# A fill of spare scratch rows moved to the end of attention, another order of that end, and twenty products of ones ahead of the first expert

## The chip, the core and the metric

The kernel runs on one core of one Trainium2 chip. The metric is the time of one execution on the device in microseconds (us), lower being better; it is given as the median of several executions. Inside the core, TensorE (PE in the views, with PEld for its weight loads), VectorE (DVE), ScalarE (ACT) and GpSimd (POOL) compute, each from an instruction queue of its own; SyncE (SP) only issues transfers here. Sixteen DMA engines carry the transfers.

## The reference

Three stages, each fed by the one before. Cut to what matters:

```python
# 1. attention as a chunked scan: batch 4, heads 8, length 768, head size 32, state 16, chunk 32
for c in range(24):
    L = np.exp(cum[..., :, None] - cum[..., None, :]) * causal
    M = np.einsum('bhin,bhjn->bhij', Cc, Bc) * L
    y[:, :, sl] = einsum(M, xc) + einsum(Cc, state) * exp(cum)
    state = decay_full * state + sum_j(Bx)
x = y.transpose(0, 2, 1, 3).reshape(3072, 256)          # 3072 tokens of 256 values
# 2. and 3. two layers of 8 experts; each token goes to the one expert of its largest logit
for e in range(8):
    h = np.maximum(x[mask_e] @ w1[e], 0.0)               # 256 -> 1024
    out[mask_e] = gate_w[mask_e, None] * (h @ w2[e])     # 1024 -> 256
```

The first layer takes its logits from normalised tokens and expert embeddings, the second from `x @ w_gate`.

## The kernel before

**Attention.** The work is cut into eight "quads" q = 0..7 (two for each batch, four heads each). A quad has an `intra` part (products within a chunk, three groups of them), a state part, and an `inter` part (what the states add, again three groups, the last step of each being the copy of `y` from PSUM to `yT`). One Python program writes all instructions in an order made by hand: quad q's `intra` is interleaved with quad q-1's `inter`, and generators (`run(gen, n)` advances one by n steps) put other work between. An engine runs its own instructions in the order in which they were written; semaphores order the engines against each other.

**Routing.** `batch_route` computes the gate of one batch, or of half a batch, and calls `route`: on PE the rank of each token in its expert ("rk" tiles, a sum over `cum`, the running count by expert), on DVE the slot number `idx` and the new `cum`, and on POOL one indirect DMA for each 128 tokens (L218), which scatters 266-word rows to the slots of the expert in DRAM scratch: `scr1` for the first layer, `scr2` for the second. The `idx` tiles have two buffers. At the end of attention there are four such halves: `p0` and `p1` of batch 2, `parts[0]` and `parts[1]` of batch 3.

**Fills.** Slots that no token reaches must hold an id out of range. `prefill` (L259) writes the tile `zrow` over them by DMAs on SP: `scr1` in the quad q = 1, `scr2` in q = 2 to 5. For each expert of `scr2` there are two blocks: 384 rows (399 KB) and behind them 256 overflow rows (266 KB). `scr2` gets its first scatter in the first layer.

**End of attention and early block.** The first 162 rows of expert 0 (`early1`, tiles ending in m0a) go through the first layer in plain f32 while attention ends: transposes, eight products h0 to h7, then y0 and y1, its gate and its rank `rkm0a`. `counts` (L239) sums `cum` by a PE product `cntm`; its program position is behind the last rank of batch 3.

**First layer.** `xrm` is the load of expert 0's other 270 rows from `scr1` (L279); it waits for all scatters to `scr1`. Then PE transposes these rows (`xT0m`, `xT1m`, L289), ACT and DVE split them into a high and a low part (`xhm`, `xlm`), and each weight product is made of three (L308 for h, L330 for y). The experts follow one after another, then the second layer in the same way. `wsplit` (L120 on ACT, L121 on DVE) splits a weight tile; `wload` issues weight loads on SP.

Of the kernel before, what the change touches and what calls it, by code (L numbers as in the profile page):

```python
# [9 lines left out]
F32 = mybir.dt.float32  # L10
# [10 lines left out]
NTOK, D, E, F = NB * S, 256, 8, 1024  # L21
# [7 lines left out]
C2P, C2T, X2T = 128, 3, 2  # L29
R1 = NTOK + 384  # L30
R2 = NTOK + 512
# [5 lines left out]
def ssm_moe_moe_kernel(  # L37
# [20 lines left out]
    pe, dve, act, pool, sp = nc.tensor, nc.vector, nc.scalar, nc.gpsimd, nc.sync  # L58
# [8 lines left out]
    scr2 = dram.tile([E * R2, W], F32, name="scr2")  # L67
# [22 lines left out]
    def wload(upto):  # L90
        while wpos["load"] < min(upto, len(pieces)):
            i = wpos["load"]
            m, e, which, k = pieces[i]
            if m == 1 and e < NEE and which == 0:
                raw = fpool[0].tile([128, WP], F32, name=f"raw{i}")
            else:
                raw = wpool0.tile([128, WP], F32, tag="raw", name=f"raw{i}", bufs=3)
            sp.dma_start(raw, wsrc[m][which][e, :, k * WP:(k + 1) * WP])
            wraw[i] = raw
            if m == 1 and e < NEE and which == 0:  # L100
                eraw[e].append(raw)
            wpos["load"] += 1
# [26 lines left out]
    ones = const.tile([128, 128], BF16, name="ones")  # L129
# [126 lines left out]
                reason="rows come from all scatters",  # L256
            )

    def prefill(scr, r, blocks, es):  # L259
        for e in es:  # L260
            o = e * r
            for pn, n in blocks:
                sp.dma_start(
                    scr[o:o + pn * n, :].rearrange("(p t) w -> p t w", t=n),
                    zrow[:pn].to_broadcast([pn, n, W]),
                )
                o += pn * n
# [253 lines left out]
    with ExitStack() as actx:  # L521
# [30 lines left out]
        def load_br(b):  # L552
            t = fil_p.tile([128, 4, NCH, NS], F32, tag="brt", name=f"brt{b}")
            sp.dma_start(t, br[b])
            return t
# [83 lines left out]
        def fil(n):  # L639
            for _ in range(n * rate):  # L640
                next(fil_gen, None)
                run(side, 1)
                run(router, steps)
# [3 lines left out]
        def warm(n):  # L647

            nwarm[0] += 1
            p = psC.tile([128, 512], F32, tag="c", name=f"pw{nwarm[0]}")  # L650
            for _ in range(n):
                pe.matmul(p, lhsT=wz[:, :128], rhs=wz, start=True, stop=True)
# [33 lines left out]
        def quad_p(q):  # L686

            b, hq = divmod(q, 2)
            p = psC.tile([128, 512], F32, tag="c", name=f"pp{q}")
            pe.matmul(p[:, :384], lhsT=selA[64:128, 128 * b:128 * b + 128],  # L690
                      rhs=asp[64:128, 384 * hq:384 * hq + 384], start=True, stop=True,
                      tile_position=(64, 0))
            pv = p[:, :384].rearrange("p (v i) -> p v i", i=CH)
            if q == NQ - 2:
                return pv
            t = au.tile([128, 6, CH], F32, tag="pt", name=f"pt{q}")
            act.copy(t, pv)
            return t

        def quad_c(q, r):  # L700

            pr = slice(32 * r, 32 * r + 32)
            eng = pool if q in (1, 2, 3) else dve
            eng.tensor_tensor(cxb[q % 2][pr, :, r, :], cxs[q][pr], pts[q][pr], ALU.mult)

        def quad_f(q):
            fb = au.tile([128, NS, NCH], F32, tag="fb", name=f"fb{q}")
            act.copy(fb, ft[:, q:q + 1, :].to_broadcast([128, NS, NCH]))
            return fb
# [20 lines left out]
        def quad_state(q, us, fb):  # L730
            st = au.tile([128, NS, NCH], F32, tag="st", name=f"st{q}", bufs=1)
            dve.tensor_tensor_scan(
                st[:].rearrange("p n c -> p (n c)"), fb[:].rearrange("p n c -> p (n c)"),
                us[:].rearrange("p n c -> p (n c)"), 0.0, op0=ALU.mult, op1=ALU.add,
            )
            sx = au.tile([128, NCH, 2, NS], F32, tag="sx", name=f"sx{q}")
            sv = st[:].rearrange("p n c -> p c n")
            act.activation(sx[:, :, 0, :], sv, AF.Copy, scale=hmask[:, 0:1])
            dve.tensor_scalar(sx[:, :, 1, :], sv, hmask[:, 1:2], None, op0=ALU.mult)
            return sx  # L740

        def quad_transpose(q, sx):
            ss = au.tile([128, 3, 128], F32, tag="ss", name=f"ss{q}")
            p = psC.tile([128, 512], F32, tag="c", name=f"sT{q}")
            for g in range(3):
                pe.transpose(
                    p[:, 128 * g:128 * g + 128],
                    sx[:, 4 * g:4 * g + 4].rearrange("p c h n -> p (c h n)"), ident[:]
                )
            pv = p[:, :384].rearrange("p (g m) -> p g m", m=128)  # L750
            act.copy(ss[:, 0:1], pv[:, 0:1])
            act.copy(ss[:, 1:], pv[:, 1:])
            return ss
# [58 lines left out]
        def run(gen, n=None):  # L812

            while gen is not None and (n is None or n > 0):
                if next(gen, "end") == "end":
                    return
                n = None if n is None else n - 1
# [210 lines left out]
        for q in range(1, NQ - 2):  # L1028
            b, hq = divmod(q, 2)
            rate = 2 if q == 1 else 1  # L1030
            steps = 2
            cur = Quad(q)
            if q == 1:
                prefill(scr1, R1, [(C1P, C1T)], range(4))
                pts[0] = quad_p(0)
                for r in range(4):
                    quad_c(0, r)
                warm(2)
                fil(1)
                run(cs)  # L1040
                warm(2)
                pend.fb = quad_f(0)
            sx = quad_state(q - 1, pend.us, pend.fb)
            cur.intra(0)
            fil(1)
            pts[q] = quad_p(q)
            pend.ss = quad_transpose(q - 1, sx)
            fil(1)
            if q + 3 < NQ and q > 1:
                halves[q + 3] = expand_half(q + 3, raws[q + 3])  # L1050
            quad_c(q, 3)
            if q + 4 < NQ and q > 1:
                raws[q + 4] = load_half(q + 4)
            fil(1)
            if q == 1:
                halves[4] = expand_half(4, raws[4])
                raws[5] = load_half(5)
            quad_c(q, 1)
            cxs[q + 1] = cxs.get(q + 1) or load_cx(q + 1)
            pend.inter(0)  # L1060
            quad_c(q, 2)
            cur.fb = quad_f(q)
            pend.inter(1)
            fil(1)
            quad_c(q, 0)
            xts[q + 1] = dma_x(q + 1)
            if q < NQ - 3:
                fil(2)
            cur.intra(2)
            pend.inter(2)  # L1070
            if hq == 0:
                run(router)
                rows = new_rows(b - 1)
                router = batch_route(b - 1, (yTs[q - 2], yTs[q - 1]), rows, 0, NT, 5)
            fil(3 if q < NQ - 3 else 0)
            if hq == 0 and b + 2 < NB:
                brs[b + 2] = load_br(b + 2)
            cur.intra(1)
            if q == 1:
                prefill(scr1, R1, [(C1P, C1T)], range(4, 8))  # L1080
            else:
                prefill(scr2, R2, [(C2P, C2T), (C2P, X2T)], ((0, 1), (2, 3, 4), (5, 6), (7,))[q - 2])
            pend = cur

        q = NQ - 2
# [21 lines left out]
        early = early1()  # L1107
# [15 lines left out]
        run(p0, 1)  # L1123
        quad_c(q + 1, 3)
        wload(7)
        run(p0, 1)
        c6.inter(1)
        c7 = Quad(q + 1)
# [20 lines left out]
        run(p0)  # L1149
        c7.inter(1)  # L1150
        run(p1, 1)
        run(early, 1)
        run(p1, 2)
        c7.inter(2)
        rows = new_rows(NB - 1, act.copy)
        parts = [
            batch_route(NB - 1, (yTs[NQ - 2], yTs[NQ - 1]), rows, t0, t0 + 3) for t0 in (0, 3)
        ]
# [3 lines left out]
        run(p1, 1)  # L1162
        run(parts[0], 3)
        run(p1)
        run(early, 1)
        run(parts[1], 2)
        run(parts[0], 1)
        run(early, 1)
        run(parts[1], 1)
        run(early, 1)  # L1170
        run(parts[0], 1)
        run(parts[1], 1)
        run(parts[0])
        run(early, 2)
# [16 lines left out]
    with ExitStack() as c1:  # L1191
        psM = c1.enter_context(tc.tile_pool(name="psM", bufs=2, space=PSUM))
# [46 lines left out]
        prev = route(C0P, C0T, None, va0[:C0P], 1, rows0[:C0P], scr2, E * R2, scats2, psM, "m0a")  # L1239
        for _ in prev:  # L1240
            pass
        for k in range(KD):
            x_split_k(xr, pn, nt, xs, k, psM, "c", "m0")

# [4 lines left out]
        for e in range(E):  # L1249
            tag = f"m{e}"  # L1250
# [64 lines left out]
    psM = ctx.enter_context(tc.tile_pool(name="psM2", bufs=2, space=PSUM))  # L1315
# [5 lines left out]
    for e in range(E):  # L1321
        tag = f"n{e}"
# [95 lines left out]
```

## Time and profile before

| what | value |
|---|---|
| median of 3 executions | 503.15 us (501.55, 503.15, 503.8) |
| the profiled execution | 503.57 us, its span 501.9 us |
| granted TensorE clock, mean | 0.968 |
| PE busy | 460.2 us (92%) in 3207 instructions |
| PE weight loads | 410.9 us (82%) |
| DVE busy | 287.1 us (57%) |
| ACT busy | 239.7 us (48%) |
| POOL busy | 138.5 us (28%) |
| fill DMAs `scr<-zrow` | 8 of 448.9 KB, 8 of 399.0 KB, 8 of 266.0 KB |

The span runs from the first to the last instruction of the profiled execution; the 1.67 us between it and that execution's time lie around it. Busy shares are means over stages that differ. The granted clock is PE's share of full speed: 1.00 is 2.4 GHz, 0.5 is 1.2 GHz.

### The profile page before, as it was taken

To read this page: it belongs to the slowest core of one execution; us is meant where nothing else is said; L and a number is where in the kernel's file an instruction comes from. 1 tells how busy PE (TensorE), PEld (TensorE's weight loads), DVE (VectorE), ACT (ScalarE), POOL (GpSimd) and SP (SyncE) were. 2 spreads that over 40 slices of the span, in tenths; PEclk is the share of its full clock that TensorE was granted. 3 is DMA by queue.
4 is the path that set the end of the run, shared out by engine and by line. 5 is a ranking of instruction groups with operands and counts; after the bars stand their busy time and mean duration, and the time that the engine had idled before them with its cause. 6 is when DMAs were issued, how large, how long until landed. Compare 5 with 4: busy or idle time off the path is not lost.

```text
span 501.9 us, 8953 instructions
## 1 busy us (share of the span) xinstructions
PE 460.2 (92%) x3207; PEld 410.9 (82%) x3209; DVE 287.1 (57%) x682; ACT 239.7 (48%) x558; POOL 138.5 (28%) x211
## 2 busy tenths in 40 slices
PE   8889987989759999999999999899999999999992
PEld 3555754767659999999999999789999999999991
DVE  6977775787736837456383746543666357244330
ACT  5542533556625644547364545344556346344330
POOL 6334465155830030321303030511101210212011
PEclk9997978989979999999999999999999999999997
DMA  7267899586224535252433535252754564411000
GB/s 247 84 189 195 219 214 260 131 259 208 77 87 138 194 100 194 84 178 101 154 128 111 168 110 194 71 153 92 236 183 153 170 229 145 131 39 60 22 22 16
DMA packets 50212, 72.09 MB, mean 144 GB/s; under 512 B 23870, under 2 KB 36093, under 8 KB 49899
## 3 DMA queue, kind: packets, MB, share of 16 engines
q1 hardware_dynamic: 45595, 61.66, 41.2%
q0 software_dynamic: 4560, 9.70, 5.8%
q8 instruction: 32, 0.52, 0.4%
q14 instruction: 25, 0.20, 0.1%
HBM read 52.53 MB, written 19.74 MB: 144 GB/s over the span
## 4 chain that ended last, share of the span: by engine, by line
PE 47%; DMA 21%; issue 13%; DVE 9%; POOL 3%; ACT 2%; POOLq 1%; SPq 1%; another core or an unknown queue 1%; DVEq 0%; ACTq 0%
DMA out_dram<-os0n,idsn 13%; PE y1m L330 7%; PE y0m L330 7%; DMA out_dram<-os0n1a,idsn1a 6%; PE cb L604 4%; DVE lt L581 2%; PE h0m L308 2%; PE y L759 2%; PE h1m L308 2%; PE h6m L308 2%; PE h2m L308 2%; PE h7m L308 2%; PE h5m L308 2%; PE h3m L308 2%; PE h4m L308 2%
## 5 line engine op out<-in xcount | busy, mean ns | idle before, releaser
L218 POOL DMA_INDIRECT scr<-rows2m,idxm x31 | 31.4, 1014 | 129.8 <-DVE cum L215 106.4
L121 DVE TENSOR_TENSOR w0l<-raw,w0h 128x1024 fp32r<-128x1024 f32 x30 | 36.7, 1224 | 10.2 <-ACT w0h L120 10.2
L121 DVE TENSOR_TENSOR w1l<-raw,w1h 128x1024 fp32r<-128x1024 f32 x30 | 36.4, 1218 | 0.9 <-ACT w1h L120 0.9
L604 PE MATMUL cb<-cw,btt 128*128 128x256 f32 x96 | 32.4, 445 | 1.7 <-ACT btt L549 0.8
L218 POOL DMA_INDIRECT scr<-rows,idxa x24 | 26.4, 1098 | 20.4 <-DVE cum L215 10.3
L120 ACT CAST w1h<-raw 128x1024 fp32r<-128x1024 f32 x30 | 31.5, 1052 | 0.0
L437 POOL DMA_INDIRECT out_dram<-os0n,idsn x8 | 7.8, 969 | 85.6 <-DVE idsn L431 44.6
L120 ACT CAST w0h<-raw 128x1024 fp32r<-128x1024 f32 x30 | 31.2, 1042 | 0.0
L581 DVE TENSOR_TENSOR_SCAN lt<-ab,ipat 128x512 f32<-128x512 f32 x24 | 29.2, 1219 | 1.7 <-PE ab L578 1.5
L312 DVE SCALAR_TENSOR_TENSOR hln<-h0n,hhn 128x384 fp32r<-128x384 f32 (+1 forms) x8 | 4.2, 524 | 43.8 <-ACT hhn L311 39.9
L611 DVE TENSOR_TENSOR mb<-cb,lt 128x256 f32<-128x256 f32 x48 | 18.0, 417 | 14.4 <-PE cb L604 8.5
L604 PEld LDWEIGHTS cb<-cw,btt 128*128 128x128 f32 x96 | 18.0, 212 | 10.0 <-PE y L759 2.3
L330 PE MATMUL y1m<-hhm,w1h 128*128 128x432 f32 (+1 forms) x64 | 23.0, 360 | 0.0
L330 PE MATMUL y0m<-hhm,w1h 128*128 128x432 f32 (+1 forms) x64 | 22.9, 358 | 0.0
L312 DVE SCALAR_TENSOR_TENSOR hlm<-h0m,hhm 128x432 fp32r<-128x432 f32 (+1 forms) x8 | 4.7, 587 | 31.6 <-issue 23.4
L330 PE MATMUL y0m<-hhm,w1l 128*128 128x432 f32 (+1 forms) x64 | 22.4, 349 | 0.0
L330 PE MATMUL y1m<-hhm,w1l 128*128 128x432 f32 (+1 forms) x64 | 22.3, 349 | 0.0
L330 PE MATMUL y0m<-hlm,w1h 128*128 128x432 f32 (+1 forms) x64 | 22.3, 348 | 0.0
L330 PE MATMUL y1m<-hlm,w1h 128*128 128x432 f32 (+1 forms) x64 | 22.3, 348 | 0.0
L592 POOL TENSOR_TENSOR mb<-brt,lt 128x128 f32<-128x128 f32 x24 | 10.6, 440 | 40.3 <-DVE lt L581 35.7
L335 ACT COPY ytm<-y1m 128x432 f32<-128x432 f32 (+1 forms) x8 | 4.0, 502 | 31.8 <-PE y1m L330 31.8
L716 PEld LDWEIGHTS y<-mb,xbd 128*64 128x64 f32 x384 | 15.8, 145 | 4.0 <-issue 2.1
(607 smaller groups left out, 1568.6 us busy)
## 6 DMA issues: line engine op xcount, KB each, us to landing
raw<-in_m2w_dram SPq DMA_DIRECT2D x32, 512.0 KB
raw<-in_m1w_dram SPq DMA_DIRECT2D x28, 512.0 KB
scr<-zrow SPq DMA_DIRECT2D x8, 448.9 KB
scr<-zrow SPq DMA_DIRECT2D x8, 399.0 KB
xrm<-scr SPq DMA_DIRECT2D x7, 448.9 KB
xrn<-scr SPq DMA_DIRECT2D x6, 399.0 KB
xbd<-in_xs__dram SPq DMA_DIRECT2D x24, 96.0 KB
scr<-zrow SPq DMA_DIRECT2D x8, 266.0 KB
```

Of the source, the lines that this page charges most:

```text
L120: act.copy(hi[:, sl], raw)
L121: dve.tensor_tensor(lo[:, sl], raw, hi[:, sl].bitcast(F32), ALU.subtract)
L218: i = pool.indirect_dma_start(out=scr[:], out_offset=bass.IndirectOffsetOnAxis(ap=idx[:pn, t, :], axis=0), in_=rows[:, t, :W], in_offset=None,
L308: pe.matmul(p[:, :n], lhsT=w[:, o:o + 128], rhs=x[:, kd, :n], start=(k == 0), stop=(k == 5))
L312: dve.scalar_tensor_tensor(hl[:, f, :n], p[:, :n], 0.0, hh[:, f, :n].bitcast(F32), op0=ALU.max, op1=ALU.subtract,)
L330: pe.matmul(p[:, :n], lhsT=w[:, o:o + 128], rhs=h[:, f, :n], start=(k == 0), stop=(k == 3 * KF - 1))
L581: dve.tensor_tensor_scan(lts[b, g][:, 2 * v:2 * v + 2].rearrange("p u c i -> p (u c i)"), p, ipat[:].rearrange("p c i -> p (c i)"), 0.0, o ...
L592: pool.tensor_tensor(m[:, :, :, 64:80], brs[b][:, us_, 4 * g:4 * g + 4], lt[:, us_, :, CH - 1:CH].to_broadcast([128, 2, 4, NS]), ALU.mult,)
L604: pe.matmul(p[:, cc], lhsT=btt[:, c].rearrange("p h j -> p (h j)"), rhs=ctt[:, :, c * CH:(c + 1) * CH], start=True, stop=True)
L611: dve.tensor_tensor(mbs[2 * b + hq, g][:, :, o:o + 2, :64].rearrange("p u c i -> p c u i"), p[:, :, us_, :], lts[b, g][:, us_, o:o + 2, :] ...
L716: pe.matmul(yps[g][64 * hs:64 * hs + 64, r * 80:r * 80 + 80], lhsT=xts[hs][:, c, :], rhs=mbs[q, c // 4][:, hs, c % 4, :], start=(r == 0), ...
L759: pe.matmul(yps[g][64 * hs:64 * hs + 64, :320].rearrange("p (c w) -> p c w", w=80)[:, :n, :64], lhsT=ss[:, g, 64 * hs:64 * hs + 64], rhs=c ...
```

## The change

Three edits. The 256-row block of all eight experts of `scr2` is no longer filled in quads 2 to 5, but in one go behind `wload(7)`. At the end of attention `c7.inter(2)` comes before two steps of `p1`, two steps of the early block go, and two steps (of the early block and of `parts[0]`) change places. And twenty products of ones, whose result nothing reads, stand on PE behind `rkm0a` and ahead of the transposes of `xrm`.

```diff
-    def prefill(scr, r, blocks, es):
+    def prefill(scr, r, blocks, es, first=0):
         for e in es:
-            o = e * r
+            o = e * r + first
...
-                prefill(scr2, R2, [(C2P, C2T), (C2P, X2T)], ((0, 1), (2, 3, 4), (5, 6), (7,))[q - 2])
+                prefill(scr2, R2, [(C2P, C2T)], ((0, 1), (2, 3, 4), (5, 6), (7,))[q - 2])
...
         wload(7)
+        prefill(scr2, R2, [(C2P, X2T)], range(E), C2P * C2T)
         run(p0, 1)
...
         run(p1, 1)
-        run(early, 1)
+        c7.inter(2)
         run(p1, 2)
-        c7.inter(2)
         rows = new_rows(NB - 1, act.copy)
...
         run(p1)
-        run(early, 1)
         run(parts[1], 2)
         run(parts[0], 1)
         run(early, 1)
         run(parts[1], 1)
+        run(parts[0], 1)
         run(early, 1)
-        run(parts[0], 1)
         run(parts[1], 1)
...
+        p = psM.tile([128, 4, 128], F32, tag="a", name="pw")
+        for _ in range(20):
+            pe.matmul(p, lhsT=ones, rhs=ones[:].unsqueeze(1).to_broadcast([128, 4, 128]),
+                      start=True, stop=True)
         for k in range(KD):
             x_split_k(xr, pn, nt, xs, k, psM, "c", "m0")
```

On SP, in quad 3 (the names: `xbd` is x of a quad, `cxt` its C, `scr_69` the second layer's scratch), before the change:

```order
L680 DMA xbd_121<-in_xs__dram 64x12x32 x2
L263 DMA scr_69<-zrow 384x1x266
L263 DMA scr_69<-zrow 256x1x266
L263 DMA scr_69<-zrow 384x1x266
L263 DMA scr_69<-zrow 256x1x266
L263 DMA scr_69<-zrow 384x1x266
L263 DMA scr_69<-zrow 256x1x266
L564 DMA cxt_1032<-in_cx_dram 128x384
L680 DMA xbd_122<-in_xs__dram 64x12x32 x2
```

With the change only the three blocks of 384 rows stay between the loads of x and of C. The others stand on SP behind the weight loads of the end of attention (`raw` is a weight tile; `xrm0a` is the load of the early block, `xrm` that of expert 0's other rows):

```order
L279 DMA xrm0a<-scr_68 81x532
L98 DMA raw_1382<-in_m1w_dram 128x1024
L98 DMA raw_1384<-in_m1w_dram 128x1024
L98 DMA raw_1386<-in_m1w_dram 128x1024
L263 DMA scr_69<-zrow 256x1x266 x8
L279 DMA xrm_1823<-scr_68 90x798
```

Before the change `xrm` stood directly behind the third weight load.

On PE, where attention ends, the order before (`rka_3` is the rank of `parts[1]`, `cntm` the sum of `cum`, the rest the early block):

```order
L197 MATMUL rka_3_1720<-oha_3_1712,tri 128x24
L378 MATMUL h6m0a<-xm0a,cw 128x162 x2
L378 MATMUL h7m0a<-xm0a,cw 128x162 x2
L242 LDWEIGHTS ones
L242 MATMUL cntm_1753<-cum_79,ones 1x8
L244 LDWEIGHTS ones
L244 MATMUL cntm_1753<-hole_86,ones 1x8
L389 MATMUL y0m0a<-hm0a,cw 128x162 x8
```

And with the change:

```order
L197 MATMUL rka_3_1712<-oha_3_1704,tri 128x24
L378 MATMUL h4m0a<-xm0a,cw 128x162 x2
L378 MATMUL h5m0a<-xm0a,cw 128x162 x2
L242 LDWEIGHTS ones
L242 MATMUL cntm_1745<-cum_79,ones 1x8
L244 LDWEIGHTS ones
L244 MATMUL cntm_1745<-hole_86,ones 1x8
L378 MATMUL h6m0a<-xm0a,cw 128x162 x2
L378 MATMUL h7m0a<-xm0a,cw 128x162 x2
L389 MATMUL y0m0a<-hm0a,cw 128x162 x8
```

The early block has fallen two h products back: h6 and h7, which stood ahead of `cntm`, now stand behind it. The orders of DVE and POOL are the same in both kernels; on ACT the last copies of `y` to `yT` come ahead of the exponentials of `p1`. The twenty products of ones stand on PE between `rkm0a` and the first transpose of `xrm`, each with a weight load of its own.

## Rows read from the trace of the kernel before

**Rows 1.** The page: granted TensorE clock in 40 slices.

```profile
PEclk9997978989979999999999999999999999999997
```

**Rows 2.** Windows: from:to, length, busy by engine (instructions), clock, DMA share, GB/s.

```profile
core 0: us, PE busy (x) PEld busy (x) DVE busy (x) ACT busy (x) POOL busy (x), PEclk, DMA share, GB/s
77.00:83.00 6.00, 2.82 (x22) 1.60 (x18) 1.28 (x3) 1.47 (x5) 3.95 (x5) 1.00 1.14 239
83.00:91.00 8.00, 7.59 (x51) 5.34 (x52) 7.05 (x13) 3.91 (x15) 1.77 (x4) 0.79 1.02 252
124.00:131.00 7.00, 5.63 (x48) 4.91 (x47) 5.41 (x35) 4.47 (x18) 5.95 (x7) 1.00 0.22 82
131.00:139.00 8.00, 6.02 (x43) 5.58 (x44) 5.88 (x13) 4.72 (x9) 6.63 (x8) 1.00 0.24 85
139.00:145.00 6.00, 1.28 (x8) 0.98 (x7) 0.88 (x7) 0.33 (x1) 2.89 (x7) 0.72 0.42 115
145.10:148.50 3.40, 3.40 (x14) 3.21 (x15) 1.27 (x3) 0.80 (x3) 0.89 (x5) 0.50 0.18 68
148.50:152.00 3.50, 3.50 (x31) 3.50 (x31) 2.62 (x5) 3.50 (x8) 0.00 (x0) 1.00 0.02 5
```

**Rows 3.** Timeline of PE, DVE and ACT around 80 us: start, busy, [idle before <-releaser].

```profile
79.18 0.60 PE L604 MATMUL cb<-cw,btt 128*128 128x256 f32 x2
83.41 1.78 PE L759 MATMUL y<-cxb,ss 128*64 128x256 f32 x8 [3.21 <-ACT ss L751]
...
82.66 0.76 DVE L611 TENSOR_TENSOR mb<-cb,lt 128x256 f32<-128x256 f32 x2 [4.16 <-remote]
...
82.62 0.48 ACT L697 COPY pt<-pp 128x384 f32<-128x384 f32 x1 [1.19 <-remote]
```

**Rows 4.** Timeline of SP, the issues of transfers.

```profile
69.96 4.71 SPq L263 DMA_DIRECT2D scr<-zrow  x6
77.21 5.21 SPq L680 DMA_DIRECT2D xbd<-in_xs__dram  x4
...
116.12 1.29 SPq L98 DMA_DIRECT2D raw<-in_m1w_dram  x3
...
140.65 2.38 SPq L279 DMA_DIRECT2D xrm<-scr  x2
```

**Rows 5.** Timeline of POOL: the scatters.

```profile
73.47 1.25 POOL L218 DMA_INDIRECT scr<-rows,idxa  x1 [0.73 <-DMA scr<-zrow]
...
80.44 0.97 POOL L218 DMA_INDIRECT scr<-rows,idxa  x1 [0.30 <-issue]
...
126.84 0.98 POOL L218 DMA_INDIRECT scr<-rows,idxa  x1 [0.30 <-issue]
...
133.66 1.96 POOL L218 DMA_INDIRECT scr<-rows,idxa  x1 [0.30 <-DVE w0l L121]
...
137.20 0.97 POOL L218 DMA_INDIRECT scr<-rows,idxa  x1 [0.30 <-issue]
```

**Rows 6.** The chain that ended last, at 137 us: the last scatter's flight.

```profile
137.20 3.12 DMA scr<-rows,idxa
```

**Rows 7.** Timeline of DVE: the slot numbers of the last half batch.

```profile
130.08 0.18 DVE L206 TENSOR_REDUCE idxa<-psa 128x3 int32<-128x24 f32 x1
```

**Rows 8.** Who waited for scatters of the tile `idxa` from 120 to 140 us (us, times).

```profile
  DVE idxm0a L206: 0.8, 1
```

**Rows 9.** Timeline of PE from 129 to 150 us.

```profile
129.25 0.71 PE L378 MATMUL h7m0a<-xm0a,cw 128*128 128x162 f32 x4
130.68 0.17 PE L242 MATMUL cntm<-cum,ones 128*1 128x8 bf16 x1 [0.71 <-DVE cum L215]
130.87 2.47 PE L389 MATMUL y0m0a<-hm0a,cw 128*128 128x162 f32 x16
139.00 0.18 PE L197 MATMUL rkm0a<-ohm0a,tri 81*81 81x16 bf16 x1
143.90 0.68 PE L289 MATMUL xT0m<-ident,xrm 90*128 90x90 f32 x3 [4.71 <-DMA scr<-rows,idxm0a]
149.11 0.29 PE L308 MATMUL h3m<-xhm,w0h 128*128 128x270 f32 x1
```

**Rows 10.** Timeline of PE at the start: products of 512 columns.

```profile
1.30 4.43 PE L652 MATMUL pw<-wz 128*128 128x512 bf16 x11 [1.30 <-DVE wz L826]
6.33 1.25 PE L652 MATMUL pw<-wz 128*128 128x512 bf16 x5
```

## The prediction

> **What bounds the kernel now.** I began with the page's line of granted clock [rows 1]. PE is the engine with most work, and its clock is near full in all slices but one inside and some in attention, so the time is made of PE's work plus the places where PE stands still. What the change touches ends by about 150 us of the span; behind that PE is busy without a gap until the last expert, so whatever is won or lost up to the start of the first expert's steady products (h3 at 149.11 [rows 9]) is won or lost at the end, one to one.
>
> I then cut the stretches that the change touches into windows [rows 2]. Two are weak. From 77 to 83 us PE is busy 2.82 of 6 us, DVE 1.60, ACT 1.47, while the DMA share is 1.14, which is more than full. From 139 to 145 us PE is busy 1.28 of 6 us: attention has ended and the first expert's rows aren't there yet. The timeline says what each engine waited for. Around 80 us [rows 3] DVE waits 4.16 us and ACT 1.19 us for something that the profile can only call remote, and PE 3.21 us for ACT. At the same time SP needs 5.21 us to issue four small loads, just behind six fills that took 4.71 us to issue [rows 4], and POOL sends six scatters between 73.47 and 81.41 us [rows 5]. So three compute engines, SP and the queues stand together, in the one place where fills and scatters meet. At 140 us the order is simpler: the last scatter is issued at 137.20 and flies 3.12 us [rows 6], to 140.32; `xrm` is loaded from 140.65 [rows 4], and its transposes start at 143.90 after 4.71 us of idle PE [rows 9]. The clock has dropped by then: 0.50 in the window 145.10 to 148.50, 1.00 from 148.50 [rows 2].
>
> **Part 1: the fill moves.** Eight DMAs of 266 KB, 2.13 MB, leave quads 2 to 5; three of quad 3's six go. Its fills come to 3 x 399 = 1.20 MB in place of 1.20 + 0.80 = 2.00 MB. At the 239 GB/s of the window [rows 2] the 0.80 MB are 3.3 us of transfer, and the queue in front of the scatters and loads is that much shorter. What the stall is worth: by PE its 3.21 us of idle [rows 3], and a little more in front of it, since the products at 79.18 end at 79.78 and the next work starts at 83.41, 3.63 us later. By DVE at most 4.16 us, of which it would have waited some anyway, since PE's products that feed L611 end at 79.78 and it restarts at 82.66: 2.88 us. I take 3.3 us, between 2.9 and 3.6; the clock at 0.79 behind the stall [rows 2] speaks for the upper half. Below, this term is nothing, if the stall doesn't come from the amount of fill; the row nearest to it, 3.3 us of transfer gone against 3.3 us of stall, speaks for all of it. **Term: -3.3 us.** The Trainium skill, "SBUF — State Buffer", section "SBUF: two separate sides", speaks against this: the engines' ports and the DMA ports of SBUF can't contend with each other. By it the engines were held by something else than the fill's traffic and this term is 0; the trace, with three engines, SP and the queues standing at once, leaves that open, and it is the first rival.
>
> The fill now stands on SP behind three weight loads that took until 117.41 to issue [rows 4]. Ahead of it nothing is late; behind it on SP stands only `xrm`, which can't go before 140.65 anyhow. Issuing six fills took 4.71 us, so eight take some 6.3 us, and 2.13 MB at 239 GB/s take 8.9 us: until about 132 us if the weights land near 123. That ends 8 us ahead of `xrm`, and the window 124 to 131 has a DMA share of 0.22 [rows 2], so there is room. The first scatter to `scr2` comes behind `rkm0a`, so it doesn't wait.
>
> What is late is the scatters to `scr1` that fly meanwhile. DVE's slot numbers of `parts[1]`, at 130.08 [rows 7], write the tile that `p1`'s scatters read (two buffers); the last of these starts at 126.84 [rows 5] and with a flight of 3.12 us [rows 6] lands at 129.96. So the slack is 0.12 us, and the same wait shows as 0.8 us one route later [rows 8]. A scatter that shares the queues with the fill lands later. Below that is 0; above, the 4.16 us that DVE stood in the crowded window [rows 3]. I take half, **2.1 us**. DVE is then 2.1 us late at L206, and the new `cum` behind it too. The last scatters themselves have 3.6 us in hand: they start at 133.66 at the earliest, behind the others in POOL's queue and behind a weight split of DVE [rows 5].
>
> **Part 2: the order.** Two h tiles, h6 and h7, fall behind `cntm`, which waits for `cum` (0.71 us, at 130.68 [rows 9]). In the kernel before they lay in DVE's shadow. A pair of them costs 0.71 us [rows 9], and pipelined 1.25 us for both by my estimate. So between `cntm` and y0, which start at 130.68 and 130.87, stand 1.25 us more. From there to the end of `rkm0a`, 139.00 + 0.18 = 139.18, the early block's steps follow from each other, with PE 6.02 us busy of 8 from 131 to 139 [rows 2]. `rkm0a` then ends at 139.18 + 1.25 = 140.4, or with the late L206 at 142.5. The other moves change PE alone at places where POOL and DVE set the pace (POOL 5.95, DVE 5.41 of 7 us in 124 to 131): nothing, at most 0.3 us either way.
>
> **Part 3: the ones.** The rows at the start of the kernel have the same shape: five in 1.25 us, 0.25 us each with the last one's way through the array in it, and eleven in 4.43 us, 0.40 us each [rows 10]. 512 columns at 2.4 GHz are 0.213 us; I take 0.217 for a warm PE, **20 x 0.217 = 4.34 us**, and the second row as the bound, 20 x 0.40 = 8.1 us, if PE's clock is low there. Where `rkm0a` ends at 139.18 they would fit into the 4.71 us of idle [rows 9] at no cost. But it ends at 140.4 or 142.5, and they run to 144.7 or 146.85, past 143.90. What they give: the clock doesn't drop. From 143.90 to h3 took 5.21 us (149.11 - 143.90). The 3.40 us in the window at 0.50 would take 1.70 at full clock, so 3.5 us. h3 then starts at 144.7 + 3.5 = 148.2 (0.9 us earlier) without the delay, at 146.85 + 3.5 = 150.35 (1.2 us later) with it. The point where it turns is transposes at 145.6. **Term: +1.2 us.**
>
> **The sum** against the profiled execution, 503.57 us (0.42 above the median of the runs shown): 503.57 - 3.3 + 1.2 = 501.5 us. A run differs from the median by up to 1.6 us, so I call 0.5%, 2.5 us, what can be told from no change.
>
> **The rivals.**
> 1. The stall at 80 us stays, as the SBUF page's rule would have it: the scatters or the loads of x, both still there, hold the engines. For it: only some of the stretches with crowded queues show this wait, and 1.20 MB of fill are still in the queue. Against: it begins as the fills have been issued and ends as the share falls. 503.57 + 1.2 = 504.8 us. Chance 0.20.
> 2. The stall goes, and the scatters land on time, since the share at 124 to 131 is only 0.22 and a scatter is small: 503.57 - 3.3 - 0.9 = 499.4 us. Chance 0.26.
> 3. The stall stays and the scatters land on time: 503.57 - 0.9 = 502.7 us. Chance 0.12.
> 4. Slower: the stall moves with the fill. 2.13 MB now meet the scatters of `p0`, `p1` and `parts` at 124 to 132 us, as 2.00 MB met them at 74 to 81. DVE is then not 2.1 but 4.2 us late at L206 (the wait of [rows 3]), `rkm0a` ends at 140.4 + 4.2 = 144.6, the ones at 148.9 and h3 starts at 152.4, 3.3 us later than now: with the -3.3 of the first stall, no change. But PE then stands 0.7 + 4.2 = 4.9 us in front of `cntm`, and behind 4.71 us of idle the clock was at 0.50 [rows 2, 9]. y0 with 2.47 us [rows 9] and y1 of the same size would take up to 4.9 us more, half of that if the clock comes back half way: 503.57 + 2.5 = 506 us, 508.5 at the worst. It decides from transposes later than 145.6 + 3.3 = 148.9 us. Against: here the queues hold little else. Chance 0.12.
>
> **How the numbers follow.** The forecast, stall gone and scatters late, has the remaining 0.30: 501.5 us. The range: down, rival 2 with the stall at 3.6 us and 0.8 us of scatter between runs, 498.0; up, rival 1 with the same 0.8, 505.6. That leaves out rival 4 and a little of rival 2. Around 501.5 with half of the delay's bounds (2.1 us either way), a third lies below 500.65, the half-per-cent line: 0.10 of the 0.30. Faster: 0.26 + 0.10 = 0.36. Slower: rival 4's 0.12 and a quarter of rival 1, 0.17. Same: 0.47. Of one sign alone, the likeliest case has 499.5 to 503.5.
>
> **What would show it.** Part 1 is right if the window 77 to 83 has PE busy for most of it and the wait for "remote" is gone; wrong if DVE's wait there stays over 3 us. The delay shows as a DVE wait for a scatter in front of L206 of `parts[1]`, against 0.12 us of slack now. Part 2: `rkm0a` near 142.5 less what part 1 gave (139.2); at 137.1 there is no delay. Part 3: granted clock 1.00 from the ones through h0 to h2, and transposes that start right behind the ones and not behind `xrm`. I am wrong if the ones take 0.4 us each, if PE stands in front of `cntm` for more than 3 us, or if a stall like that at 80 us comes up at 124 to 132.

## The result, and the profile after

The changed kernel is about 1% slower: 509.21 us median of 5 executions (506.69 to 510.9) against 503.8 of before (5 executions), ratio 1.0111 with a 95% interval of 1.0069 to 1.0152. Run again later (`e9_after_again`, 12 executions against 29), the ratio was 1.0075 (1.0048 to 1.0103). Medians are of all executions; a few executions fell in a slower state with a lower granted clock, and the ratios leave these out. The forecast was 501.5 us, its range ended at 505.6.

The profiled execution after took 506.69 us (span 504.7), 3.1 us more than that of before. Its windows over the stretches of [rows 2], in the same columns:

```profile
77.00:83.00 6.00, 4.28 (x37) 2.59 (x36) 5.06 (x10) 2.99 (x11) 4.59 (x8) 1.00 1.20 260
83.00:91.00 8.00, 7.27 (x69) 6.11 (x70) 6.18 (x13) 4.10 (x17) 2.19 (x3) 1.00 0.39 86
...
117.00:124.00 7.00, 4.53 (x38) 4.11 (x37) 4.43 (x29) 3.96 (x18) 4.77 (x5) 1.00 1.09 302
124.00:131.00 7.00, 1.85 (x16) 1.56 (x16) 2.61 (x16) 0.84 (x3) 3.12 (x4) 0.67 0.89 217
131.00:139.00 8.00, 8.00 (x39) 7.98 (x39) 4.30 (x6) 4.58 (x7) 5.73 (x7) 0.65 0.15 54
139.00:145.00 6.00, 4.28 (x28) 2.65 (x27) 2.49 (x15) 1.45 (x4) 0.40 (x1) 1.00 0.45 127
```

The weak stretch at 77 to 83 us is gone: DVE is busy 5.06 us in place of 1.60. A new one stands at 124 to 131: PE 1.85 us in place of 5.63, DVE 2.61 in place of 5.41, with the DMA share at 0.89 in place of 0.22. The clock is then 0.65 from 131 to 139, where it was 1.00.

What DVE waited for in the new stretch, from its timeline (L206 is the slot number `idx` of a half batch):

```profile
117.36 0.17 DVE L206 TENSOR_REDUCE idxa<-psa 128x3 int32<-128x24 f32 x1
...
123.63 0.18 DVE L206 TENSOR_REDUCE idxa<-psa 128x3 int32<-128x24 f32 x1 [2.15 <-DMA scr<-rows,idxa]
...
130.32 0.18 DVE L206 TENSOR_REDUCE idxa<-psa 128x3 int32<-128x24 f32 x1 [3.83 <-DMA scr<-rows,idxa]
```

DVE stood twice, 2.15 + 3.83 = 5.98 us, until scatters had landed whose `idx` tile the next slot numbers overwrite. The chain shows the flight of the second of these:

```profile
121.38 8.86 DMA scr<-rows,idxa
```

8.86 us, where a flight took 3.12 in [rows 6]. The eight fills had been issued on SP from 112.14 to 121.10, just ahead of it:

```profile
110.47 0.30 SPq L279 DMA_DIRECT2D xrm0a<-scr  x1
110.82 1.28 SPq L98 DMA_DIRECT2D raw<-in_m1w_dram  x3
112.14 8.96 SPq L263 DMA_DIRECT2D scr<-zrow  x8
139.69 2.42 SPq L279 DMA_DIRECT2D xrm<-scr  x2
```

The first line also shows the gain: the early block's load is issued at 110.47 us, in the kernel before at 115.77. PE's timeline shows the end, to be held against [rows 9]:

```profile
130.90 0.17 PE L242 MATMUL cntm<-cum,ones 128*1 128x8 bf16 x1 [4.51 <-DVE cum L215]
131.00 0.16 PE L244 MATMUL cntm<-hole,ones 1*1 1x8 bf16 x1
131.09 1.45 PE L378 MATMUL h6m0a<-xm0a,cw 128*128 128x162 f32 x4
132.33 1.29 PE L378 MATMUL h7m0a<-xm0a,cw 128*128 128x162 f32 x4
133.41 3.96 PE L389 MATMUL y0m0a<-hm0a,cw 128*128 128x162 f32 x16
...
142.81 4.48 PE L1243 MATMUL pw<-ones 128*128 128x512 bf16 x20
147.13 0.40 PE L289 MATMUL xT0m<-ident,xrm 90*128 90x90 f32 x3
...
150.75 0.28 PE L308 MATMUL h3m<-xhm,w0h 128*128 128x270 f32 x1
```

PE stands 4.51 us in front of `cntm`, then h6, h7 and y0 run at the lower clock (h7 1.29 us in place of 0.71, y0 3.96 in place of 2.47), then the ones take 4.48 us. The transposes start right behind them at 147.13, though `xrm` was issued at 139.69. h3 starts at 150.75: 5.3 us ahead at 111 us, 1.6 us behind at 150.

### The profile page after: what moved, and what is told of

It reads as the page before. It is cut to its first block, busy times and chain, and to the rows that moved or that the text cites. A ratio compares the mean times of both kernels' runs of the same rounds, so it can differ in the third digit from the quotient of the medians.

```text
span 504.7 us, 8988 instructions
## 1 busy us (share of the span) xinstructions
PE 462.0 (92%) x3227; PEld 412.6 (82%) x3229; DVE 287.7 (57%) x682; ACT 240.1 (48%) x558; POOL 138.4 (27%) x211
## 4 chain that ended last, share of the span: by engine, by line
PE 48%; DMA 22%; issue 13%; DVE 10%; POOL 2%; ACT 2%; another core or an unknown queue 1%; POOLq 1%; DVEq 0%; ACTq 0%
DMA out_dram<-os0n,idsn 13%; PE y1m L330 7%; PE y0m L330 7%; DMA out_dram<-os0n1a,idsn1a 6%; PE cb L604 3%; DVE lt L581 3%; PE pw L652 2%; PE h0m L308 2%; PE h6m L308 2%; PE h1m L308 2%; PE h7m L308 2%; PE h5m L308 2%; PE h4m L308 2%; PE h3m L308 2%; PE h2m L308 2%
## 5 line engine op out<-in xcount | busy, mean ns | idle before, releaser
L121 DVE TENSOR_TENSOR w0l<-raw,w0h 128x1024 fp32r<-128x1024 f32 x30 | 36.7, 1225 | 10.2 <-ACT w0h L120 10.2
L121 DVE TENSOR_TENSOR w1l<-raw,w1h 128x1024 fp32r<-128x1024 f32 x30 | 36.4, 1216 | 1.0 <-ACT w1h L120 1.0
L604 PE MATMUL cb<-cw,btt 128*128 128x256 f32 x96 | 29.7, 413 | 1.9 <-DVE mb L611 0.9
L218 POOL DMA_INDIRECT scr<-rows,idxa x24 | 24.6, 1024 | 24.0 <-DVE cum L215 14.3
L604 PEld LDWEIGHTS cb<-cw,btt 128*128 128x128 f32 x96 | 16.5, 194 | 9.2 <-PE y L759 2.6
L716 PE MATMUL y<-mb,xbd 128*64 128x80 f32 x384 | 18.0, 241 | 1.8 <-issue 1.8
```

Source lines behind the costliest of these rows:

```text
L121: dve.tensor_tensor(lo[:, sl], raw, hi[:, sl].bitcast(F32), ALU.subtract)
L218: i = pool.indirect_dma_start(out=scr[:], out_offset=bass.IndirectOffsetOnAxis(ap=idx[:pn, t, :], axis=0), in_=rows[:, t, :W], in_offset=None,
L604: pe.matmul(p[:, cc], lhsT=btt[:, c].rearrange("p h j -> p (h j)"), rhs=ctt[:, :, c * CH:(c + 1) * CH], start=True, stop=True)
L716: pe.matmul(yps[g][64 * hs:64 * hs + 64, r * 80:r * 80 + 80], lhsT=xts[hs][:, c, :], rhs=mbs[q, c // 4][:, hs, c % 4, :], start=(r == 0), ...
```

## The experiments

Fourteen runs, each with 6 to 12 executions. Ratios are to the kernel before on the same chip. The name of a run is its label.

**First question: is it the late fill's effect on the scatters, or the order?** `e1_fill_back` puts the fill of the changed kernel back into the quads:

```diff
-                prefill(scr2, R2, [(C2P, C2T)], ((0, 1), ...)[q - 2])
+                prefill(scr2, R2, [(C2P, C2T), (C2P, X2T)], ((0, 1), ...)[q - 2])
...
-        prefill(scr2, R2, [(C2P, X2T)], range(E), C2P * C2T)
```

> The changed kernel with its fill back in quads 2 to 5; the new order and the ones stay. Theory A (the late fill keeps the scatters of p0 and p1 in flight, 8.86 us for one of them, so that DVE stands at the slot numbers and PE at cntm): the waits of 2.15 and 3.83 us in front of L206 are gone, PE waits under 1.5 us in front of cntm, the stall at 80 us is back; the transposes of xrm start near 144.7 us and h3 near 148.2, and the time is about 502.7 us against 503.6 of before, ratio 0.995 to 1.002. Theory B (the new order itself, h6 and h7 behind cntm, costs the time): PE still waits over 3 us in front of cntm or y0 runs at half clock, ratio over 1.005.

500.12 us, ratio 0.9978 (0.995 to 1.0006). The waits in front of L206 are gone and PE waits 0.98 us in front of `cntm`. So the order and the ones without the late fill don't make it slower. The transposes started at 146.00, not 144.7: y0 took 3.11 us (clock 0.87 from 131 to 139 us) and the ones 6.03 (0.72 from 139 to 145). The stall at 80 us, expected back, didn't come: DVE is busy 5.13 of 6 us from 77 to 83, and stands 3.66 us at 101 instead.

`e2_fill_only` does the reverse, the moved fill alone in the kernel before.

> The kernel before with the fill alone moved. Theory A: the load of the early block is issued near 110.5 us in place of 115.8, DVE again waits some 6 us in two pieces in front of L206, PE waits in front of cntm with h6 and h7 already done, so over 5 us, y0 at half clock; without the ones the time is 505 to 510 us, ratio 1.003 to 1.012. Theory B (order): no loss, the 5 us of attention are kept, about 499 us, ratio under 0.995.

502.27 us, ratio 1.0027 (1.0004 to 1.005). The early block's load came at 111.35; DVE waited 5.80 us in front of L206, in one piece, and PE 6.14 in front of `cntm`. The loss is a little under the expected range. In the profile what attention gained is nearly all lost before the first expert: the load is 4.42 us earlier than in the kernel before, h3 at 148.59 only 0.52. The 0.27% beyond that can't be placed in it.

`e3_idx6` leaves the fill where the change put it and gives `idx` six buffers in place of two, so that DVE has nothing to wait for. The order of instructions is the same on every engine.

```diff
-        idx = rt.tile([128, NT, 1], I32, tag="idx", name="idx" + tag)
+        idx = rt.tile([128, NT, 1], I32, tag="idx", name="idx" + tag, bufs=6)
```

> The changed kernel with six buffers in place of two for the slot numbers idx, nothing else. Theory A: DVE no longer waits for a scatter to land in front of L206, the last scatter is issued some 6 us earlier than at 133.41, cntm runs near 125 us without the 4.51 us of idle PE, y0 stays at full clock; xrm still can't be loaded before the last scatter has landed behind the fill, near 135 us. The ones end near 141 us, h3 starts near 145 in place of 150.75: about 501 us in the profile, ratio 0.990 to 1.000. Theory C (the crowded queues hold the engines whatever the buffers): DVE or POOL stands elsewhere for 4 us or more between 117 and 132 us, ratio still over 1.005.

496.85 us, ratio 0.9918 (0.9882 to 0.9954). In its timeline of DVE L206 waits for nothing, though the DMA share from 124 to 131 us is 1.10, higher than after the change:

```profile
117.38 0.17 DVE L206 TENSOR_REDUCE idxa<-psa 128x3 int32<-128x24 f32 x1
121.40 0.17 DVE L206 TENSOR_REDUCE idxa<-psa 128x3 int32<-128x24 f32 x1
124.55 0.17 DVE L206 TENSOR_REDUCE idxa<-psa 128x3 int32<-128x24 f32 x1
```

This settles it against theory C: the queues are as crowded (scatters issued from 113 to 128 us land 7.1 to 9.4 us later), and DVE and PE run on, because DVE no longer needs the tile that a scatter still reads. This one number turns 0.75% slower into 0.8% faster (ratios from two chips). `e7_before_idx6` is the control, the six buffers alone in the kernel before.

> The kernel before with six idx buffers alone, a control. In the kernel before the last scatter of p1 lands 0.1 us ahead of the slot numbers that overwrite its tile, and one wait of 0.8 us is left at idxm0a, off the path. Theory A (the buffers only matter while the fill keeps the scatters in flight): no change, ratio 0.997 to 1.002. Rival (the buffers help anywhere): ratio under 0.995.

504.43 us, ratio 1.0008 (0.998 to 1.0036): nothing, as expected. The buffers only pay where the fill delays the scatters.

`e4_ones_only` adds the twenty products of ones to the kernel before.

> The kernel before with the twenty products of ones alone. They fit into the idle 4.71 us of PE: rkm0a ends at 139.2, the ones at 143.5, xrm is there at 143.9. By the prediction's part 3 the granted clock is then 1.00 through h0 to h2 and h3 starts 1.7 us earlier than 149.11: about 502 us, ratio 0.994 to 0.999. If the ones don't keep the clock, or run at 0.40 us each and end at 147, the ratio is 1.000 to 1.008.

499.97 us, ratio 0.9971 (0.9947 to 0.9995): as part 3 of the prediction has it. PE's timeline:

```profile
138.33 0.18 PE L197 MATMUL rkm0a<-ohm0a,tri 81*81 81x16 bf16 x1
138.37 4.48 PE L1244 MATMUL pw<-ones 128*128 128x512 bf16 x20
143.31 0.42 PE L289 MATMUL xT0m<-ident,xrm 90*128 90x90 f32 x3 [0.46 <-DMA xrm<-scr]
```

The ones end 0.46 us before `xrm` is there, the granted clock from 139 to 145 us is 1.00 (0.72 before), and from transposes to h3 it takes 146.97 - 143.31 = 3.66 us in place of 5.21.

**Second question: what do ones and order cost where the fill is late?** On one chip, beside the changed kernel itself (`e9_after_again`):

> The changed kernel once more, as a measure for the three beside it. All theories: slower than before, ratio 1.006 to 1.015, with waits in front of both L206 of p1 and parts[1] or one of them, together near 6 us.

505.47 us, ratio 1.0075 (1.0048 to 1.0103), with waits of 1.35 and 5.92 us in front of L206. `e10_after_no_ones` takes the ones out of the changed kernel:

> The changed kernel without the twenty products of ones. In its trace the ones end at 147.1 us, xrm's data were there near 142.7 (issue 139.69 and 3.0 of flight). If the ones stand on the path (theory D): transposes at 142.8, h3 5.2 us behind at half clock, 148 in place of 150.75: 2.5 us less, ratio 0.5% below that of the changed kernel. If what they give in clock is worth as much (theory E): within 0.2% of it.

503.01 us, ratio 1.0028 (1.0002 to 1.0054), 0.47% below the changed kernel, with intervals that just overlap. Its transposes start at 143.16, right behind `rkm0a`, and h3 at 148.75; in `e9_after_again` they start at 147.67 and 151.30. Here are the starts, `e9_after_again` first:

```profile
141.67 6.17 PE L1243 MATMUL pw<-ones 128*128 128x512 bf16 x20
147.67 0.40 PE L289 MATMUL xT0m<-ident,xrm 90*128 90x90 f32 x3
...
143.16 0.60 PE L289 MATMUL xT0m<-ident,xrm 90*128 90x90 f32 x3 [0.43 <-PE rkm0a L197]
```

The same twenty products that give 0.3% in the kernel before take about 0.5% here, since `rkm0a` ends too late for them to fit. `e11_old_order_fill_ones` has the late fill and the ones in the old order:

> The kernel before with the fill moved and the twenty ones, in the old order; two idx buffers. If h6 and h7 behind cntm are what the fill's delay hits (theory F, order and fill together), rkm0a ends near 140.8 as with the fill alone, 2 us ahead of the changed kernel, the ones end near 145.3 and h3 starts near 148.8: ratio 0.3 to 0.5% below the changed kernel. If the order is worth nothing here: ratio within 0.2% of the changed kernel's.

503.92 us, ratio 1.0049 (1.002 to 1.0077): 0.26% below the changed kernel, with intervals that overlap. `rkm0a` ended at 141.45, only 0.4 us earlier than in `e9_after_again` (141.81): here y0 took 4.69 us and y1 2.98. What the order costs there isn't settled.

`e5_idx6_no_ones` and `e6_idx6_ones8` vary the ones where the six buffers have taken the wait away; `e8_old_order_fill_idx6_ones8` has the old order with eight. In their round the kernel before took 504.77 us, in that of `e3_idx6` 501.68.

> The changed kernel with six idx buffers and without the twenty products of ones. With six buffers and the ones, rkm0a ended at 136.2 us, the ones took 5.99 us, and the load of xrm, issued at 134.89, had been there for some 4 us when the transposes started at 141.91. Theory D (the ones now stand on the path): the transposes start near 138, h3 near 143.2 at half clock in place of 145.5, 2.3 us less than with the ones, about 494.5 us, ratio 0.984 to 0.991. Theory E (without them the clock stays low longer and takes the gain back): within 0.5 us of the run with the ones, ratio near 0.992.

> The same with eight products of ones in place of twenty. Theory D: the eight take 1.7 to 3.4 us behind 136.1, the transposes start at 138 to 139.5 with the clock on its way up, h3 near 142.5: 0.983 to 0.990 of before, at least 2 us below the run with twenty. Theory E: eight don't raise the clock and h3 starts where it does without any.

> The kernel before with the fill moved, six idx buffers and eight products of ones, in the old order of the end of attention. If the new order costs by h6 and h7 behind cntm, y0 here starts some 2 us earlier than with the new order, rkm0a ends near 134.5, the eight ones near 136.5, and h3 starts 3.5 us behind the landing of xrm near 138: 141.5, about 492.5 us, ratio 0.979 to 0.988. If the order doesn't matter with the buffers there, it is within 0.3% of the new order with eight ones.

502.81 us, 0.9968 (0.9941 to 0.9995); 502.7 us, 0.9944 (0.9911 to 0.9978); 503.12 us, 0.9957 (0.9925 to 0.9988). All three, like `e3_idx6`, are faster than the kernel before, but none reaches the range of theory D, and that twenty are too many isn't borne out by times with the six buffers, though h3 started at 144.01 with eight and at 145.54 with twenty. The old order with eight is within 0.3% of the new one with eight, as expected of an order that doesn't matter there; the intervals are as wide as that. In `e5_idx6_no_ones` `xrm` itself was late (transposes at 140.47), with the clock at 0.51 from 139 to 145 us. In `e8_old_order_fill_idx6_ones8` PE idled 2.62 us behind the eight ones and the clock fell all the same (0.63 from 145 to 150 us). Twenty that ended 0.46 us before the data kept it (`e4_ones_only`). Whether the shorter gap or the larger number did that isn't separated.

**Third question: where should the fill stand?** `e12_fill_behind_xrm` keeps the old order, two `idx` buffers and twenty ones, and issues the 256-row fills behind the loads of `xrm` and of expert 1's rows, when the last scatter to `scr1` has landed:

```diff
         xr = load_rows(scr1[NE0:NMX, :], pn, nt, scats1, "m0")
+        xr1 = fetch1(1)
         rest(0, cnt1, NMX, scr1, R1, psM)
+        prefill(scr2, R2, [(C2P, X2T)], range(E), C2P * C2T)
...
-                nxr = fetch1(e + 1)
+                nxr = fetch1(e + 1) if e else xr1
```

> The old order, two idx buffers, twenty ones; the 256-row fills are issued behind the loads of xrm and of expert 1's rows, when the last scatter to scr1 has landed. Theory A: attention is as early as with the fill moved (early block's load near 111 us) and its end as quick as with the ones alone (31.6 us from that load to h3): h3 near 142.6, about 497 us, ratio 0.983 to 0.990. Rival: the scatters of m0a to scr2 now wait for the fill and hold POOL until about 153 us, the weight loads behind it on SP are late, and the first two experts wait: ratio over 0.994.

496.55 us, ratio 0.9889 (0.9859 to 0.992), the lowest time and the lowest ratio of all, in the range of theory A. Lines of its timelines of PE, SP and POOL:

```profile
133.97 4.48 PE L1246 MATMUL pw<-ones 128*128 128x512 bf16 x20
139.61 0.42 PE L289 MATMUL xT0m<-ident,xrm 90*128 90x90 f32 x3 [1.17 <-DMA xrm<-scr]
143.26 0.28 PE L308 MATMUL h3m<-xhm,w0h 128*128 128x270 f32 x1
...
136.05 0.76 SPq L279 DMA_DIRECT2D xrm<-scr  x2
138.48 5.75 SPq L263 DMA_DIRECT2D scr<-zrow  x8
...
154.09 1.08 POOL L218 DMA_INDIRECT scr<-rows,idxm0a  x1 [18.97 <-DMA raw<-in_m1w_dram]
```

h3 starts at 143.26, 5.9 us ahead of [rows 9]. The price that the rival named is there, POOL stands 18.97 us in front of the first scatter to `scr2`, but PE is busy 59.60 of the 60 us from 140 to 200, so PE doesn't wait for POOL there.

**Fourth question: is the order worth anything by itself?** `e13_order_only` is the new order in the kernel before, `e14_new_order_fill_behind` the new order with the fill as in the last run and eight ones.

> The kernel before with the new order of the end of attention alone; fill in the quads, no ones. Theory G (the order gives: the weight splits of DVE fall behind the last scatters): from cntm to the start of the last scatter 4.7 us in place of 6.5, the load of xrm and the transposes 1.8 us earlier, rkm0a still ahead of them; ratio 0.994 to 0.998. Theory F (the order costs, h6 and h7 behind cntm): transposes no earlier, y0 in part at half clock, ratio 1.000 to 1.005.

> The new order with the fill behind the loads of xrm and of expert 1's rows, and eight ones in place of twenty, since rkm0a ends some 9.8 us behind cntm and the data of xrm are there some 11.4 us behind it. Theory G: transposes 11.5 us behind cntm in place of 14.2 with the old order and the fill in the same place, so h3 near 141 us, 2 us below that run: ratio 0.980 to 0.987. If the order is worth nothing: ratio 0.988 to 0.994.

503.29 us, 0.9978 (0.9953 to 1.0002), and 502.32 us, 0.9947 (0.9913 to 0.9982), on a chip with 504.49 for the kernel before. In the first the last scatter started 5.24 us behind `cntm` (6.52 before) and the transposes 12.91 us behind it (13.22 before); in the second they came 14.18 us behind it, as in `e12_fill_behind_xrm` (14.17): `xrm` was issued 2.0 us sooner after `cntm`, but `rkm0a` ended 2.4 us later after it, and its eight ones took 3.44 us. It lies in neither of its expected ranges. So a small gain by the order isn't excluded and isn't shown, and together with the fill in its better place the new order wasn't better. The profile of `e13_order_only` is the fastest of its twelve executions, 3.3 us below their median.

The table has the starts that the argument uses, in us of each span, from the timelines.

| run | early block's load | `cntm` | last scatter to `scr1` | transposes | h3 | span |
|---|---|---|---|---|---|---|
| before | 115.77 | 130.68 | 137.20 | 143.90 | 149.11 | 501.9 |
| changed | 110.47 | 130.90 | 133.41 | 147.13 | 150.75 | 504.7 |
| e9_after_again | 110.43 | 130.08 | 132.59 | 147.67 | 151.30 | 502.0 |
| e2_fill_only | 111.35 | 131.15 | 137.36 | 143.21 | 148.59 | 500.1 |
| e3_idx6 | 111.08 | 125.17 | 129.90 | 141.91 | 145.54 | 498.0 |
| e4_ones_only | 115.37 | 130.00 | 136.52 | 143.31 | 146.97 | 497.9 |
| e12_fill_behind_xrm | 111.44 | 125.44 | 132.16 | 139.61 | 143.26 | 494.0 |

From h3 to the end of the span it is 350.7 to 354.4 us in the profiles of all kernels here, with no tie to the change. A single profile therefore says little on 1 us of the end, and the ratios decide. The two profiled executions of the changed kernel are 2.5 and 1.6 us faster than its medians; where its other executions lose more isn't seen. The ones took 4.48 us in one of the two and 6.17 in the other (granted clock from 139 to 145 us 1.00 and 0.75).

## Why the prediction was wrong

**Part 1, the stall: borne out.** The window 77 to 83 shows what was announced, and no kernel with the fill moved shows a wait for "remote" there (two of the five with the fill in the quads do). The term was -3.3 us. The early block's load came at 110.4 to 112.8 us in the eleven profiles with the fill moved (mean 111.35), and at 111.6 to 115.8 in the five with the fill in the quads (mean 114.20): -2.8 us, and -5.3 us between the two profiles first compared. The stall has no fixed place: in `e4_ones_only` 77 to 83 is well filled and DVE stands 4.68 us at 103 instead, and in `e13_order_only` (its fastest execution) attention was as early with the fill in the quads as without; in `e8_old_order_fill_idx6_ones8`, with the fill moved, DVE still waits 4.08 us for PE at 79. What is the same in all profiles is SP: the four loads of x behind quad 3's fills take 5.21 to 10.10 us to issue in the five with six fills ahead of them, and 2.75 to 4.09 in the eleven with three. In `e4_ones_only` the chain goes through two such loads, and PE's products start as the second lands:

```profile
77.06 10.10 SPq L680 DMA_DIRECT2D xbd<-in_xs__dram  x4
...
81.43 7.80 DMA xbd<-in_xs__dram
93.94 5.16 DMA xbd<-in_xs__dram
...
99.23 3.26 PE L716 MATMUL y<-mb,xbd 128*64 128x80 f32 x46 [0.48 <-DMA xbd<-in_xs__dram]
```

The first rival, with the rule of the Trainium skill that stood beside it ("SBUF — State Buffer", "SBUF: two separate sides"), didn't come: attention got shorter with the fill out. The rule itself isn't contradicted: in `e3_idx6` the engines ran on at a DMA share of 1.10, and the losses in front of L206 and in `e4_ones_only` came by waits for a landing, of which it says nothing. So "this term is 0" didn't follow from it. Whether the wait for "remote" was one of that kind isn't shown.

**Part 1, the delay of the scatters: the step that failed.** "I take half, 2.1 us" was the mechanism with its place (DVE at L206, two buffers, 0.12 us of slack), but mis-sized: 5.98 us measured, and 7.27 and 5.80 in `e9_after_again` and `e2_fill_only`. Even the upper bound, 4.16 us, was too low. It was taken from an engine's wait in the crowded window of before, where what counts is the flight of a scatter in such a window; the trace of before shows no landing there, so the bound had no row to stand on. The flight is 8.86 us against 3.12: one landing 5.7 us late accounts for nearly all of the 5.98. I had also looked at L206 of `parts[1]` only. The L206 of `parts[0]` waits in the same way for `p0`'s scatters, 2.15 us; that wait doesn't add to the sum, since `e2_fill_only` has 5.80 us at `parts[1]` alone.

The same in the terms of the sum, between the two profiles: from the early block's load to `cntm` it takes 5.5 us longer (20.43 against 14.91), where the prediction had 2.1; from `cntm` to the end of `rkm0a` 3.55 us longer (12.05 against 8.50), where it had 1.25 for h6 and h7 and nothing for the clock that the longer idle time costs; from there to h3 2.1 us less, as forecast. That is 6.9 us lost against 1.2 forecast, of which the 5.3 us gained in attention leave 1.6.

**Parts 2 and 3: right alone, wrong together.** Rival 4 had this chain (PE 4.9 us in front of `cntm`, the clock lost, y0 slower), with 506 us and a chance of 0.12; the profile shows 4.51 us and a y0 of 3.96 us. Its deciding point held too: it counted from attention as it was before, so with the 5.3 us added back the transposes at 147.13 stand at 152.4, beyond its 148.9 and beyond 150.9, which it becomes with 5.3 in place of 3.3. Its 506 us is near the profiled 506.69; the median, 509.21, lies beyond its worst case, and that part has no cause here. I gave it too small a chance, because the delay of 4.2 us on which it rests was my upper bound. h6 and h7 behind `cntm` were priced rightly (1.25 us forecast; 1.32 in `e13_order_only`, 9.82 against 8.50 from `cntm` to the end of `rkm0a`). The ones were priced rightly where the clock was full (4.34 us forecast, 4.48 measured; 5.99 to 6.17 in three profiles where it wasn't), and that they keep the clock is shown by `e4_ones_only`; but with the fill late they stand on the path. Without them the transposes start 4.5 us earlier and h3 only 2.6 us, since the clock gives back the rest; a gain of 0.3% became a loss of 0.5% (`e10_after_no_ones`).

**The other moves of the order: the prediction gave them nothing, "at most 0.3 us either way"; not settled.** DVE's own order is unchanged, yet its weight splits (L121) wait for casts of ACT that stand behind the copy of h7. The first starts 2.86 us behind `cntm` in `e13_order_only` (128.37 - 125.51) and 0.60 in the kernel before, so fewer of the last scatters run beside the splits. I had looked at the order of DVE and POOL, and not at the time when ACT lets the splits begin.

One sum of the range is off: rival 2's terms, 503.57 - 3.6 - 0.9 - 0.8, give 498.3 and not 498.0. Nothing hangs on it.

## What to carry to other kernels

A transfer that nobody waits for still costs where it flies beside transfers that somebody waits for: ask which tiles the delayed ones hold, and how many buffers there are, before asking what the transfer itself takes. The price of a crowded queue is a flight in a crowded window, not an engine's wait in it; where the trace shows no such flight, the bound stays open. Work that only keeps PE's clock must be fitted to the idle time that is left after the other edits: the same twenty products changed the time by -0.3% or +0.5%, and after eight that ended 2.6 us before the data the clock fell.

## What the runs showed of the hardware that was not expected

The POOL instruction of a scatter is not always 0.97 us. Beside DVE instructions that read two SBUF tiles (the weight splits L121, two instructions in a row of the view) it lasts longer; in `e2_fill_only`, timelines of DVE and POOL:

```profile
131.60 2.34 DVE L121 TENSOR_TENSOR w0l<-cw,w0h 128x1024 fp32r<-128x1024 f32 x2
133.87 2.34 DVE L121 TENSOR_TENSOR w1l<-cw,w1h 128x1024 fp32r<-128x1024 f32 x2
...
131.10 0.97 POOL L218 DMA_INDIRECT scr<-rows,idxa  x1 [4.11 <-DVE cum L215]
132.38 4.68 POOL L218 DMA_INDIRECT scr<-rows,idxa  x1 [0.30 <-issue]
```

4.68 us in `e2_fill_only` and 4.69 in `e11_old_order_fill_ones`, 1.75 and 1.96 in the kernel before [rows 5]. In the two long cases the scatter ends about 0.85 us after the last split. In all others up to 140 us that begin beside a split (1.16 to 1.97 us, in eleven profiles) it ends 2.06 to 2.08 us after the split's row began, whenever it began itself. The Trainium skill ("SBUF — State Buffer", "Who interferes with whom") has such a DVE instruction contend with GpSimd's reads, with which these rows agree, and infers that it doesn't hold up descriptor generation. What the scatter does in that time, descriptors or something else, the trace doesn't tell, so the inference stays open here.
